# Two filler groups of an attention and soft-MoE kernel divided otherwise: one matmul more, and four of 384 columns for twelve of 128

## The chip, the cores and the metric

The kernel runs on one core of one Trainium2 chip. The metric is the device time of one execution in microseconds (us). Five executions of the kernel before have a median of 302.42 us (302.04 to 304.46). One execution was taken with the hardware profiler as well.

## The reference

What must be computed is an attention over 8 batches of 12 heads (448 tokens, 64 numbers per head) with soft-capped scores, whose output goes into a soft mixture of experts:

```python
scores = cap * np.tanh(scale * np.matmul(q, k.transpose(0, 1, 3, 2)) / cap)      # cap = 30
attn = np.exp(scores - np.max(scores, axis=-1, keepdims=True))
x = np.matmul(attn / np.sum(attn, axis=-1, keepdims=True), v)                    # then tokens x 768
logits = x @ phi                                                                 # 3584 x 32 slots
d = softmax of logits over the tokens;  slot_input = d.T @ x
slot_out[e] = np.maximum(slot_input[e] @ w1[e], 0.0) @ w2[e]                     # 8 experts
c = softmax of logits over the slots;   out = c @ slot_out
```

(The softmaxes are written out in the reference; here they are told in words.) Nothing of the change touches any of these results.

## The kernel before

**Tiles and chunks.** Two heads make a pair, so there are 48 pairs; each pair has 7 key tiles, which makes 336 tiles. The main loop runs over j from 0 to NCH - 1, with NCH = 56, and each j handles a chunk of 6 tiles. For a chunk, TensorE (PE in the profile) makes the scores (`qk_chunk`, L316) into one of two PSUM buffers `sc`; ScalarE (ACT) takes the tanh from there into an SBUF tile `ex` (L325) and later the exponential in place (L329); VectorE (DVE) takes the exponential of one of the six tiles by a polynomial (L362 to L367). Two chunks later TensorE multiplies with the values (`pv_mms`, L385), and VectorE divides by the sums (`norm`, L392 and L395). GpSimd (POOL) casts the values (L286) and issues the loads of weights.

**Who sets the order.** The order on each engine is written out by hand. Every j has slots named by letters: pv_first (the first four key tiles of a pair), slot "a", pv_tail, scores of the next chunk, slot "b", pv_rest with the norm, slot "c", the second half of the next scores, slot "d". A table `aux` holds what is to be called in each slot, and `at(j, slot, f, ...)` (L542) enters a call. TensorE then takes its instructions strictly in that order.

**Fillers.** Some slots hold matmuls whose result nobody reads. `spare(n, parts)` (L547 to L549) takes a tile named `junk` in the PSUM bank that the product with the values uses as well (pool `psV`, one buffer, tag "pv"), and calls `busy` (L625 to L632):

```python
    def spare(n, parts=3):
        busy(n, psV.tile([P, parts * P], F32, name="junk", tag="pv"))
...
        if home.shape[-1] > P:
            for _ in range(n // 3):
                pe.matmul(home, ones, wide, start=True, stop=True)    # L629: 384 columns
            n, home = n % 3, home[:, 0:P]
        for _ in range(n):
            pe.matmul(home, by, by, start=True, stop=True)            # L632: 128 columns
```

So n counts blocks of 128 columns: with parts = 1 each block is a matmul of its own, with parts = 3 three blocks go into one matmul of 384 columns and the remainder into single ones. Each matmul comes with a weight load of its own. Since `junk` and `pv` share one buffer, the fillers must wait until VectorE has read the pair before (`norm`), and the next pair's product must wait until the fillers have left their results.

**Near the end of the loop.** Line 608 enters three such groups: 8 blocks in slot "d" of j = 50, 8 in slot "d" of j = 52, 12 in slot "d" of j = 54, all with parts = 1. In each, pv_first of the next j follows. After j = 54 no scores are left to be made: j = 55 has pv_first, slot "a", pv_tail and pv_rest of pair 45, and then the loop is left. The rest of the attention follows outside the loop: the products of pairs 46 (`pvm`) and 47 (`pvl`), the logits of the last batch (`lpl`), the slot sums (`slpl`). Then come the first expert layer (`hp`, L823), the second (`so_ps`, L856), whose weights are partly read back from DRAM (`w2t`, L802, on the queue of SyncE, SP), and the output (`op`, L892 and L939; stores L872).

Of the kernel before, what the change touches and what calls it, by code (L numbers as in the profile page):

```python
# [36 lines left out]
def kernel(  # L37
# [27 lines left out]
    NCH = NTILE // CH  # L65
# [476 lines left out]
    def at(j, slot, f, *a):  # L542
        if j < 0:
            j, slot = 0, "b"
        aux.setdefault((j, slot), []).append((f, a))
# [21 lines left out]
    for b in range(B):  # L567
        j, p = b * PER, 6 * b
# [36 lines left out]
        at(1 + n * (NCH - 5) // len(wjobs), "b", *job)  # L605
    for j, slot, n in ((0, "a", 10), (0, "c", 10), (1, "b", 10), (1, "c", 8)):
        at(j, slot, spare, n, 1)
    for j, slot, n, parts in ((NCH - 6, "d", 8, 1), (NCH - 4, "d", 8, 1), (NCH - 2, "d", 12, 1)):
        at(j, slot, spare, n, parts)
    at(0, "c", init_vbd, 0)  # L610
    at(1, "c", init_vbd, 1)
# [376 lines left out]
```

## Time and profile before

| what | value |
|---|---|
| median of five executions | 302.42 us (302.04 to 304.46) |
| the profiled execution: its own time | 302.04 us |
| the profiled execution: its span, first to last instruction | 300.1 us |
| mean granted TensorE clock over the span | 0.984 |
| busy: PE / ACT / DVE / POOL | 266.0 / 265.6 / 237.5 / 138.8 us |
| matmuls into `junk` of 128 columns (L632), of 384 columns (L629) | 75 and 63 |
| group of j = 50: first and last start | 227.38 and 227.78 us |
| group of j = 52: first start | 236.45 us |
| group of j = 54: first and last start | 245.49 and 246.11 us |

The profiled execution's own time is 1.94 us more than its span, which is what lies before the first and after the last instruction. A time in us with two decimals in the text below is counted from the start of the span. A busy time is the sum over the span, so it is an average over stages with different limits; which engine sets the time in one stage is read from the chain of waits and from the waits in that stage. In the timelines, a row merges neighbouring instructions of one kind: start, duration of the whole row, engine, line, operation, tiles and the number of instructions; brackets tell how long the engine was idle before and what ended that.

### The profile page before, as it was taken

What the parts mean: (1) busy time and instruction counts of PE and PEld (TensorE: products, weight loads), DVE (VectorE), ACT (ScalarE), POOL (GpSimd) and SP (SyncE); (2) the same over time, 40 slices, a digit from 0 to 9 for tenths busy, and PEclk for the clock granted to TensorE, in tenths of its full rate; (3) what the DMA queues carried; (4) which work ended last, traced back from release to release, by engine and by line L of the source; (5) the groups of instructions that cost most, each with busy time, mean ns of one, the idle gap of its engine ahead of it and who ended that gap; (6) DMA issues with size and microseconds to landing.
All of it is one profiled execution on the core that took longest, in us unless ns stands there. A gap on an engine that the chain in (4) does not pass through costs nothing.

```text
span 300.1 us, 11045 instructions
## 1 busy us (share of the span) xinstructions
PE 266.0 (89%) x4828; PEld 179.3 (60%) x4828; DVE 237.5 (79%) x497; ACT 265.6 (89%) x211; POOL 138.8 (46%) x200
## 2 busy tenths in 40 slices
PE   7898989998999999989999999899999999998710
PEld 5655556755675667566757675667666777542400
DVE  3728989898999999999899999998998864247830
ACT  4999999999999999999999999999999996237720
POOL 4583553764576456645674557465643220300000
PEclk9999999999999999999999999999999999999985
DMA  7999999999999999999999999999999479939995
GB/s 229 254 187 206 208 192 211 178 207 223 226 186 200 201 230 207 192 204 228 168 188 216 229 204 209 214 223 200 197 193 221 122 244 319 404 117 383 411 420 232
DMA packets 58560, 68.14 MB, mean 227 GB/s; under 512 B 4240, under 2 KB 54672, under 8 KB 58512
## 3 DMA queue, kind: packets, MB, share of 16 engines
q0 software_dynamic: 42448, 35.31, 76.5%
q1 hardware_dynamic: 15776, 31.89, 30.5%
q8 instruction: 38, 0.62, 0.8%
q10 hardware_dynamic: 288, 0.23, 0.2%
q14 instruction: 10, 0.08, 0.1%
HBM read 91.72 MB, written 19.27 MB: 370 GB/s over the span
## 4 chain that ended last, share of the span: by engine, by line
ACT 38%; PE 33%; DVE 14%; issue 6%; POOL 2%; DMA 2%; DVEq 0%; SPq 0%; ACTq 0%
ACT ex L325 23%; ACT ex L329 12%; PE pv L385 10%; PE sc L316 5%; DVE xq L395 3%; POOL vbd L286 2%; PE so_ps L856 2%; PE hp L823 2%; PE kps L276 2%; PE qps L276 1%; PE pv L415 1%; DVE work L364 1%; PE xps L433 1%; DVE work L362 1%; DVE work L366 1%
## 5 line engine op out<-in xcount | busy, mean ns | idle before, releaser
L325 ACT ACTIVATE ex<-sc 128x1344 bf16<-128x1344 f32 (+1 forms) x113 | 165.9, 1737 | 1.2 <-PE sc L316 1.2
L329 ACT ACTIVATE ex<-ex 128x2240 bf16<-128x2240 bf16 (+4 forms) x58 | 145.1, 2531 | 0.1
L385 PE MATMUL pv<-vbd,ex 128*128 128x130 bf16 (+1 forms) x1610 | 94.8, 211 | 8.6 <-POOL vbd L286 7.5
L385 PEld LDWEIGHTS <-ex 128*128 128x128 bf16 (+1 forms) x1680 | 76.0, 101 | 31.8 <-issue 9.1
L316 PE MATMUL sc<-qT,kT 64*64 64x448 bf16 x672 | 70.1, 359 | 2.4 <-ACT ex L325 1.8
L286 POOL CAST vbd<-vraw 64x896 bf16<-64x896 f32 x46 | 44.9, 975 | 50.8 <-PE pv L385 36.9
L366 DVE SCALAR_TENSOR_TENSOR work<-work 128x448 f32<-128x448 f32 x51 | 31.8, 623 | 1.2
L367 DVE SCALAR_TENSOR_TENSOR ex<-work 128x448 bf16<-128x448 f32 x51 | 31.9, 625 | 0.6
L365 DVE SCALAR_TENSOR_TENSOR work<-work 128x448 f32<-128x448 uint16 x51 | 31.7, 621 | 0.0
L395 DVE TENSOR_TENSOR xq<-pv,rec 128x448 bf16<-128x448 f32 x46 | 28.7, 625 | 1.6
L316 PEld LDWEIGHTS <-kT 64*64 64x64 bf16 x672 | 24.2, 105 | 7.6 <-issue 5.5
L477 POOL COPY e<-E 128x512 bf16<-128x512 bf16 x9 | 7.0, 778 | 42.9 <-PE eps L496 20.0
L364 DVE TENSOR_SCALAR work<-work 128x448 uint16<-128x448 uint16 x51 | 25.7, 504 | 0.4
L116 POOL DMA_DIRECT2D w1b<-in_moe_w_dram x32 | 24.6, 770 | 0.0
L294 POOL MEMSET vbd<- 64x1 bf16 x22 | 3.3, 149 | 43.1 <-PE pv L385 43.1
L362 DVE TENSOR_SCALAR work<-ex 128x448 int32<-128x448 bf16 x51 | 21.0, 411 | 2.1
L415 PE MATMUL pv<-ones 128*128 128x57 bf16 x502 | 20.8, 188 | 0.0
L278 DVE COPY kT<-kps 128x896 bf16<-128x896 bf16 x23 | 14.2, 618 | 7.4 <-PE kps L276 7.3
L186 POOL DMA_DIRECT2D qb<-in_q_dram x22 | 16.7, 760 | 3.4 <-DVE kT L237 3.4
L415 PEld LDWEIGHTS <-ones 128*128 128x128 bf16 x502 | 17.4, 96 | 0.4
L278 DVE COPY qT<-qps 128x896 bf16<-128x896 bf16 x23 | 14.3, 624 | 3.9 <-PE qps L276 2.9
L446 DVE COPY xT<-xps 128x896 bf16<-128x896 bf16 (+1 forms) x24 | 14.4, 600 | 3.5 <-PE xps L438 3.5
(130 smaller groups left out, 331.5 us busy)
## 6 DMA issues: line engine op xcount, KB each, us to landing
w1b<-in_moe_w_dram POOLq DMA_DIRECT2D x32, 384.0 KB, 8.4
vraw<-in_v_dram SPq DMA_DIRECT2D x44, 224.0 KB, 6.1
w2d<-in_moe_w_dram POOLq DMA_DIRECT2D x21, 384.0 KB, 8.8
w2t<-w2d SPq DMA_DIRECT2D x21, 384.0 KB, 5.6
out_dram<-ob SPq DMA_DIRECT2D x7, 768.0 KB, 8.3
qb<-in_q_dram POOLq DMA_DIRECT2D x22, 224.0 KB, 7.8
kb<-in_k_dram POOLq DMA_DIRECT2D x22, 224.0 KB, 6.4
out_dram<-obh SPq DMA_DIRECT2D x23, 192.0 KB, 2.1
```

Of the source, the lines that this page charges most:

```text
L278: dve.tensor_copy(t, ps)
L286: pool.tensor_copy(vbds[Q % 2][r, :, :, c0:c0 + DH], raw[r])
L316: pe.matmul(sc[cs, u, 0:S], qkT["k", Q][r, c, cs], qkT["q", Q][r, :, cs], start=True, stop=True)
L325: act.activation(exs[j][:, half * CS + u0:half * CS + u1, :], sc[:, u0:u1, 0:S], ACT.Tanh, scale=qk_scale / cap)
L329: act.activation(exs[j][:, u0:u1, :], exs[j][:, u0:u1, :], ACT.Exp, scale=cap)
L364: lambda: dve.tensor_scalar(b.bitcast(U16), w, 7, None, ALU.logical_shift_left),
L365: lambda: dve.scalar_tensor_tensor(p, f, p2, f, ALU.add, ALU.mult),
L366: lambda: dve.scalar_tensor_tensor(p, p, p1, f, ALU.add, ALU.mult),
L367: lambda: dve.scalar_tensor_tensor(t, p, p0, b, ALU.add, ALU.mult))
L385: pe.matmul(out_, exs[j][r, u, q0:q0 + (HP if tail else P)], v_, start=(c == 0 and g == gs[0] < NF), stop=(c == NT - 1), skip_group_check= ...
L395: dve.tensor_tensor(xq[Q][:, h, s0:s1, :], pv[:, 0:s1 - s0, 0:DH], rec.to_broadcast([P, s1 - s0, DH]), op=ALU.mult)
L415: pe.matmul(home, ones, ones[:, 0:512 - NT * W], start=False, stop=True, skip_group_check=True)
```

## The change

One line of the program is altered, in two of its three entries:

```diff
-    for j, slot, n, parts in ((NCH - 6, "d", 8, 1), (NCH - 4, "d", 8, 1), (NCH - 2, "d", 12, 1)):
+    for j, slot, n, parts in ((NCH - 6, "d", 9, 1), (NCH - 4, "d", 8, 1), (NCH - 2, "d", 12, 3)):
         at(j, slot, spare, n, parts)
```

The group of j = 50 gets a ninth matmul of 128 columns: one weight load and one matmul more. The group of j = 54 has 12 blocks as before, but in four matmuls of 384 columns instead of twelve of 128: eight weight loads and eight matmuls fewer. Together that is 14 instructions fewer on TensorE. The tile `junk` of that group is three times as wide, in the same bank. The instructions of VectorE, ScalarE, GpSimd and SyncE, their order and their waits are the same as before; the first filler of the group of j = 54 waits for VectorE, and the first product behind each group waits for TensorE's own results, in both kernels.

## The prediction

> **What bounds the kernel now.** I read the page first, for the shares, then the chain of waits in order of time around the two edited places, then the timelines of ScalarE and of TensorE there, and last the busy times by stretch up to the end.
>
> ```profile
> span 300.1 us, 11045 instructions
> PE 266.0 (89%) x4828; PEld 179.3 (60%) x4828; DVE 237.5 (79%) x497; ACT 265.6 (89%) x211; POOL 138.8 (46%) x200
> ```
>
> TensorE and ScalarE are equally full (266.0 and 265.6 us), so the page alone doesn't say which of them a filler delays. The chain of waits does (columns: start, duration, engine, tile and line):
>
> ```profile
> 227.29 0.15 PE xps L438 x2
> 227.44 0.57 PE junk L632 x8
> 228.01 0.04 issue
> 228.05 0.84 PE pv L385 x12
> ...
> 230.99 0.08 PE pv L385 x3
> 231.07 0.08 issue
> 231.14 0.94 POOL vbd L286
> 232.10 0.85 PE pv L385 x12
> ...
> 244.56 0.22 DVE rec L392
> 244.80 0.64 DVE xq L395
> 245.44 0.05 issue
> 245.49 0.86 PE junk L632 x12
> 246.35 0.04 issue
> 246.39 0.85 PE pv L385 x12
> ```
>
> Both groups are links of the chain that ended last. Between them no link belongs to ScalarE: the chain is TensorE's own sequence, broken by VectorE (244.56 to 245.44) and GpSimd (231.14 to 232.08), both of which start when a TensorE result is there. So whatever moves TensorE at 227.4 moves it at 245.5 as well. After 246.4 it is TensorE again, with one norm at 248.55, up to the first expert layer. ScalarE doesn't idle, but it doesn't hold TensorE either:
>
> ```profile
> 244.22 2.00 ACT L325 ACTIVATE ex<-sc 128x1344 bf16<-128x1344 f32 x1
> 245.39 3.16 ACT L329 ACTIVATE ex<-ex 128x2688 bf16<-128x2688 bf16 x1
> 247.73 2.00 ACT L325 ACTIVATE ex<-sc 128x1344 bf16<-128x1344 f32 x1
> 248.90 3.35 ACT L329 ACTIVATE ex<-ex 128x1344 bf16<-128x1344 bf16 x3
> ```
>
> Its last exponential ends at 252.25. The five products that need it are the last of the 30 `pvl` matmuls that run from 252.19 to 254.15, spaced about 0.06 us, so they are reached some 1.5 us after their data. TensorE has that much room to become earlier before ScalarE is the limit. The other way, a later TensorE would hurt at once, by its own sequence.
>
> **What the Trainium skill says.** Three places bear on this, all of its page "TensorE: Matmul & The Clock Gate". Its section "Back-to-back issue gap" gives a start-to-start distance of N/2.4 + 2.5 ns for N columns at the full clock: 56 ns for 128 and 162.5 ns for 384. The trace agrees: in both old groups the fillers start 55 to 56 ns apart, and 384-column fillers elsewhere (L629 at 216.52) 162 to 163 ns apart; the first step of a group is longer (66 and 174 ns). "Single matmul latency" gives (398 + N)/2.4 ns, 219 and 326 ns; the trace has 219 and 326 as the medians of the two kinds. "Part 1: The HAM clock gate (the "warmup" mystery)" says that the clock is halved after about one window of 3.4 us in which the array is idle. In this trace the granted clock is 1.00 throughout the attention and up to 286.7, and 0.50 only after TensorE has ended.
>
> **The change, part by part.** Fillers stream the same kind of data either way, so I count in columns and in matmuls.
>
> *Ninth filler at j = 50.* One more start at the distance of its neighbours: +0.056 us. Its weight load is pulled beside the filler before (the eight loads of this group lie within 227.37 to 227.82, under the matmuls). What waits behind it is the first product of the next pair, which starts at 228.05 because it needs the last filler's result to have left (275 ns after its start, which is the 219 ns of its duration and some 56 ns of waiting). So it moves by the full 0.056. Behind it the cast at 231.14 waits for TensorE, and TensorE for the cast (0.19 us idle at 232.10); both shift together. Is it hidden anywhere on the way to 245.49? The only idle of TensorE there waits for work that TensorE itself released, so I take +0.056; the ends are 0 (some wait that the profile puts down to the wrong engine covers it) and +0.07 (the first step's distance).
>
> *Four for twelve at j = 54.* Before: first filler at 245.49, first product at 246.39, so 0.900 us, of which 0.624 lie from the first to the last start (66 ns and ten times 56 ns), and 0.276 from the last start to the product. After, with the distances of the group of four at 216.52: 174 + 162 + 163 = 499 ns to the last start, and then 326 ns for the longer matmul plus the same 57 ns of waiting: 0.882 us. That is -0.018 us. The columns are the same 1536, so the array streams as long as before; what is saved is eight times 2.5 ns of distance between matmuls, and the longer last matmul moves the whole of its own extra length into the tail. The eight weight loads that go lie beside matmuls (0.67 us of loads in 245.49 to 246.2) and give nothing more. The ends: +0.02, if the first wide one starts slower, and -0.90, if the group cost nothing at all.
>
> *What doesn't change.* No other engine gets or loses an instruction or a wait, no DMA is moved, and no queue is passed. The wait that sets the group's start (VectorE's norm, 0.40 us of TensorE idle at 245.49) stays. What lies behind the group is pair 45's product, its norm (VectorE at 248.55), and the read-back of `w2t`, which began at 243.20, before the group, and whose data have landed by about 264, while the second layer reads without a wait for them. The output stage is a transfer stage:
>
> ```profile
> 266.00:268.00 2.00, 1.75 (x35) 0.83 (x25) 0.38 (x2) 0.73 (x2) 0.00 (x0) 1.00 0.04 8
> 272.00:274.00 2.00, 1.76 (x21) 0.44 (x13) 1.06 (x3) 1.58 (x3) 0.00 (x0) 1.00 1.05 392
> 282.00:284.00 2.00, 1.19 (x7) 0.58 (x6) 1.57 (x3) 1.38 (x3) 0.00 (x0) 1.00 1.02 422
> 292.00:296.00 4.00, 0.00 (x0) 0.00 (x0) 0.00 (x0) 0.00 (x0) 0.00 (x0) 0.50 1.01 422
> ```
>
> The DMA engines (last two columns: busy share and GB/s) are almost empty before the first store at 268.03 and full from 272 to 296, so the end follows the first stores, and these follow TensorE's chain: a shift at 246 arrives at the end one to one.
>
> *Sum.* +0.056 - 0.018 = +0.04 us. Against the profiled execution's own time: 302.04 + 0.04 = 302.08 us (span 300.1 + 0.04, and the same 1.94 around it). That execution is 0.38 us under the median of the five; put on the median, 302.42 + 0.04 = 302.5 us.
>
> **The rivals.** A measurement of this kernel can tell about 0.5% from no change, 1.51 us: under 300.9 is faster, over 303.9 slower.
>
> *A, the forecast:* 302.5 us. For it speak the distances, which the same trace shows for both widths, and that no wait is added.
>
> *B, slower: the granted clock falls for a window.* The place is the thinnest stretch of the attention, where TensorE is busy 1.60 of 2 us (244 to 246) and 1.66 of 2 (248 to 250), just around the altered group. If dividing the fillers otherwise put one window of 3.4 us under the monitor's bar, a window at half the clock would do 1.7 us less work, on the chain: 302.5 + 1.7 = 304.2 us. It decides from the point at which the monitor counts too little activity; the profile doesn't show that bar, but at 282 to 284 the clock is still granted in full with TensorE busy 1.19 of 2, well under the altered stretch, and the streamed columns don't fall (12 blocks remain 12, and j = 50 gains one). One of the five executions stands at 304.46, so something of that size can happen to this kernel. Little speaks for its happening because of the change.
>
> *C, faster: the group of j = 54 costs far less than its distances say.* If four wide matmuls were free, 0.90 us would go: 302.5 - 0.9 = 301.6, still within 0.5%. To be beyond, the idle of 0.40 us ahead of it and the 0.34 us ahead of `xps` at 249.47 would have to go as well (0.90 + 0.40 + 0.34 = 1.64, 300.8 us), though both wait for VectorE's norm, which nothing shortens. Against it: four such matmuls took 0.82 us at 216.52.
>
> That the change doesn't do what it says is no rival: the 14 instructions fewer are in the built program.
>
> **How the numbers follow.** A 0.77, B 0.14, C 0.09. Of C, where the gain reaches from 0.9 to 1.64 us, I put two thirds beyond 0.5% (0.06) and one third within. B's 304.2 is for a whole window on the chain, and all of it counts as slower. That gives faster 0.06, same 0.80, slower 0.14. The predicted time is A's, 302.5. The range goes down to 301.5, where the free group of C ends (302.42 - 0.90), and up to 303.8, which takes A with the spread of the executions; it leaves out B and the far part of C, 0.20 together. The unknown ends of the two edits (0 to +0.07, and -0.90 to +0.02) lie inside.
>
> **What would show it.** In the profile of the changed kernel: nine fillers of L632 at about 227.4, spaced 56 ns, with the product behind them 0.06 us later; four of L629 at about 245.5, spaced about 163 ns, each 326 ns, and the product 0.88 us after the first; a wait for VectorE ahead of the group as before, about 0.4 us; ScalarE still without idle up to 252.3; the first store at 268.1; granted clock 1.00 up to about 286.7. The prediction is wrong if the clock drops earlier, if TensorE waits in 246 to 258 for something that it didn't wait for before, or if the span differs by more than 1.5 us while these rows agree: then the time is made where I have looked for nothing, in the transfers at the end.

## The result, and the profile after

The changed kernel takes 300.87 us in the median (300.21 to 303.65, 43 runs), the kernel before in the same measurement 302.14 us (80 runs). The ratio is 0.9957, 95% interval 0.9946 to 0.9969: 1.3 us faster, where +0.04 was forecast and 301.5 was the lower end of the range.

The profiled execution took 301.26 us, its span is 299.2. First the two edited places, in the chain of waits of the changed kernel in order of time (start, duration, engine, tile and line):

```profile
227.21 0.62 PE junk L632 x9
227.84 0.04 issue
227.88 0.84 PE pv L385 x12
...
245.26 0.05 issue
245.31 0.84 PE junk L629 x4
246.15 0.04 issue
246.19 0.84 PE pv L385 x12
```

Both are still links of the chain, and both cost what their distances said. The chain's row at j = 50 begins with the second filler; in the timeline the first one starts at 227.15, so from the first filler to the product it is now 0.73 us (before, from 227.38 to 228.05, 0.68: +0.06). At j = 54 it is 0.88 us (before 0.90: -0.02). The wide fillers start 172, 163 and 162 ns apart and last 326 ns. The first store is issued at 267.98, before at 268.03, and the chain's last work on VectorE stands here:

```profile
286.37 0.66 PE op L939 x3
287.03 0.02 issue
287.06 1.02 DVE ob L946
288.07 0.92 DVEq L983
```

Before, that last copy started at 287.11. The two executions differ by up to 0.23 us at places on the way (227.15 against 227.38 already ahead of the first edited group), but from the first store to the last copy they are within 0.06 us of each other. So the span's difference is made after the last copy, while only the stores are still running. The busy times by stretch show it (the last two columns are the busy share of the DMA engines and GB/s). The kernel before:

```profile
295.00:296.00 1.00, 0.00 (x0) 0.00 (x0) 0.00 (x0) 0.00 (x0) 0.00 (x0) 0.50 0.99 409
296.00:297.00 1.00, 0.00 (x0) 0.00 (x0) 0.00 (x0) 0.00 (x0) 0.00 (x0) 0.50 0.66 264
297.00:298.00 1.00, 0.00 (x0) 0.00 (x0) 0.00 (x0) 0.00 (x0) 0.00 (x0) 0.50 0.09 36
298.00:299.00 1.00, 0.00 (x0) 0.00 (x0) 0.00 (x0) 0.00 (x0) 0.00 (x0) 0.50 0.03 12
```

The changed kernel:

```profile
296.00:297.00 1.00, 0.00 (x0) 0.00 (x0) 0.00 (x0) 0.00 (x0) 0.00 (x0) 0.50 0.79 316
297.00:298.00 1.00, 0.00 (x0) 0.00 (x0) 0.00 (x0) 0.00 (x0) 0.00 (x0) 0.50 0.04 14
298.00:299.00 1.00, 0.00 (x0) 0.00 (x0) 0.00 (x0) 0.00 (x0) 0.00 (x0) 0.50 0.00 0
```

In both, nearly all stores have landed by about 297. One engine of sixteen is a share of 0.06, so what is left behind that is the work of one engine or two: before, the packets' own times have the last ones following each other every 0.117 us, as on a single engine, until 298.56; now the last ends at 297.28. The landings of the last store say the same. There are sixteen of them: before, fourteen had come by 297.09, one came at 297.91 and one at 298.89; now fifteen have come by 297.25 and one comes at 298.05. One is late in both, but the last of all comes 0.84 us earlier, which is the difference of the spans (300.05 and 299.21). What the DMA engines carried more before is in the page's list of DMA queues. The kernel before, and then the changed one:

```profile
DMA packets 58560, 68.14 MB, mean 227 GB/s; under 512 B 4240, under 2 KB 54672, under 8 KB 58512
...
q8 instruction: 38, 0.62, 0.8%
```

```profile
DMA packets 58559, 68.12 MB, mean 228 GB/s; under 512 B 4240, under 2 KB 54672, under 8 KB 58512
...
q8 instruction: 37, 0.61, 0.8%
```

One packet less in all, and it is one of queue 8, kind "instruction": 16 KB. The experiments below show that these are TensorE's own instructions: their number and times move with the number of TensorE's instructions alone. In the trace of before the 38th starts at 286.33 and takes 0.93 us, in the midst of the stores; in the trace after, the last one is the 37th, at 267.77, when the engines are almost empty. The Trainium skill has both halves of this: "Runtime: NRT & Kernel Launch", section "Instruction fetch mechanics", says that an engine's instructions are refilled in blocks of 16 KiB, 256 instructions, by a DMA queue of the sequencer's own; "DMA: Bandwidth & Descriptors", section "Queues, rings and completion order", says that each DMA engine takes turns between its queues, packet by packet. The first agrees with the trace (9686 TensorE instructions in the program and 38 fetches, 255 for each). The second can't be read from these traces: their packets don't name their engine, so that the fetch and the late end of the stores are on the same engine is inferred from the times, not shown. The first page adds that the cost of crossing a block's boundary is "mostly hidden"; here the stores beside the fetch pay for it.

### The profile page after: what moved, and what is told of

It reads as the page before. It is cut to its first block, busy times and chain, and to the rows that moved or that the text cites. A ratio compares the mean times of both kernels' runs of the same rounds, so it can differ in the third digit from the quotient of the medians.

```text
span 299.2 us, 11031 instructions
## 1 busy us (share of the span) xinstructions
PE 266.4 (89%) x4821; PEld 179.1 (60%) x4821; DVE 237.4 (79%) x497; ACT 265.6 (89%) x211; POOL 138.8 (46%) x200
## 4 chain that ended last, share of the span: by engine, by line
ACT 39%; PE 34%; DVE 14%; issue 6%; POOL 2%; DMA 1%; DVEq 0%; ACTq 0%
ACT ex L325 23%; ACT ex L329 12%; PE pv L385 10%; PE sc L316 5%; DVE xq L395 3%; POOL vbd L286 2%; PE so_ps L856 2%; PE hp L823 2%; PE kps L276 2%; PE op L939 2%; PE qps L276 2%; PE pv L415 1%; DVE work L364 1%; PE xps L433 1%; DVE work L362 1%
```

## The experiments

Theory 1: the gain is the one fetch that no longer falls among the stores. Theory 2: it is the new shape of the fillers and what follows from their place on the chain. Theory 3: it comes from the ninth filler. The number of TensorE instructions in the program is given for each kernel; before has 9686, the changed one 9672 (each trace has records of two fewer). The filler entries of j = 0 and j = 1 stand at L606 (10, 10, 10 and 8 blocks in single matmuls); moving blocks between single and wide matmuls there changes the number of instructions, far from the end, at nearly the same streaming time.

**e1, the ninth filler alone (9688).**

```diff
-((NCH - 6, "d", 8, 1), (NCH - 4, "d", 8, 1), (NCH - 2, "d", 12, 1))
+((NCH - 6, "d", 9, 1), (NCH - 4, "d", 8, 1), (NCH - 2, "d", 12, 1))
```

> The kernel before with the ninth filler at j = 50 alone: 2 TensorE instructions more than before. Theory 1 (the gain is one 16 KB fetch of TensorE's instructions less, which in the trace of before falls at 286.33 us among the last stores): the fetch is still there, 38 fetches, no gain, +0.06 us of chain, ratio 1.000 to 1.001. Theory 2 (the gain comes from where the fillers stand and how the later transfers fall, a shift of the chain): this part costs +0.06 us, so the same ratio; the run is the control for the others. Theory 3 (the gain is this part's, by a wait that the ninth filler covers): ratio 0.996.

Measured: 302.32 us, ratio 1.0005 (0.9987 to 1.0023), 38 fetches, the last at 284.44. Theory 3 falls.

**e2, the wide group alone (9670).**

```diff
-(NCH - 2, "d", 12, 1)
+(NCH - 2, "d", 12, 3)
```

> The kernel before with the four wide fillers at j = 54 alone: 16 TensorE instructions less than before. Theory 1: 37 fetches, the whole gain, ratio 0.995 to 0.997. Theory 2: the whole gain too, if it is this part that shifts the chain. Theory 3: no gain, 1.000.

Measured: 301.18 us, ratio 0.9964 (0.9942 to 0.9986), 37 fetches. The gain belongs to this part; Theories 1 and 2 both allow that.

**e3, the kernel before with 14 instructions less at the start (9672).**

```diff
-    for j, slot, n in ((0, "a", 10), (0, "c", 10), (1, "b", 10), (1, "c", 8)):
-        at(j, slot, spare, n, 1)
+    for j, slot, n, parts in ((0, "a", 10, 3), (0, "c", 10, 1), (1, "b", 10, 1), (1, "c", 7, 1)):
+        at(j, slot, spare, n, parts)
```

> The kernel before with both groups near the end untouched, and 14 TensorE instructions less in the first 10 us of the loop: ten fillers of 128 columns at j = 0, slot a, put into three wide ones and one, and one filler less at j = 1, slot c. Theory 1: 37 fetches, the whole gain, ratio 0.995 to 0.997, and no last straggling stores after 297.4 us. Theory 2: the groups at the end are as before, so no gain: 0.999 to 1.001.

Measured: 301.01 us, ratio 0.9966 (0.9943 to 0.9989), 37 fetches within the span. The whole gain is there with the two edited groups untouched. Its last stretch is empty from 297 on:

```profile
296.00:297.00 1.00, 0.00 (x0) 0.00 (x0) 0.00 (x0) 0.00 (x0) 0.00 (x0) 0.50 0.32 128
297.00:298.00 1.00, 0.00 (x0) 0.00 (x0) 0.00 (x0) 0.00 (x0) 0.00 (x0) 0.50 0.00 0
```

**e4, the changed kernel with 14 instructions more at the start (9686).** The six fillers ahead of the loop and the four at j = 2 as single matmuls, and one filler more at j = 1.

```diff
-    spare(6)
+    spare(6, 1)
...
-            at(j + 2, "d", spare, 4)
+            at(j + 2, "d", spare, 4, 1)
...
-(1, "c", 8)
+(1, "c", 9)
```

> The changed kernel with 14 TensorE instructions added early: the six fillers ahead of the loop and the four at j = 2 as single ones of 128 columns instead of wide ones, and one filler more at j = 1, slot c. It has as many TensorE instructions as the kernel before, and the change at j = 50 and j = 54 is in it. Theory 1: 38 fetches again, the gain is gone, ratio 0.999 to 1.002. Theory 2: the gain stays, 0.995 to 0.997.

Measured: 302.12 us, ratio 0.9990 (0.9971 to 1.0010), 38 fetches, the last at 286.14. The gain is gone with the change in place. Theory 2 falls.

**e8, the kernel before with 8 instructions less at the start (9678).**

```diff
-    for j, slot, n in ((0, "a", 10), (0, "c", 10), (1, "b", 10), (1, "c", 8)):
-        at(j, slot, spare, n, 1)
+    for j, slot, n, parts in ((0, "a", 10, 1), (0, "c", 10, 1), (1, "b", 10, 1), (1, "c", 8, 3)):
+        at(j, slot, spare, n, parts)
```

> The kernel before with 8 TensorE instructions less, early (the eight fillers of j = 1, slot c, as two wide ones and two single ones). Theory 1: the last fetch is due at a fixed place in the instructions, about 14 before the end of the kernel before, so 8 less don't take it away: 38 fetches, the last of them some 8 instructions nearer to the end, no gain, ratio 0.999 to 1.001. A gain in proportion to the instructions would be 8/14 of the whole, 0.9975.

Measured: 302.10 us, ratio 1.0000 (0.9978 to 1.0021), 38 fetches, the last at 287.99. So the gain is a step, between 9678 and 9672 instructions. The traces show why: the 38th fetch starts when TensorE has begun 9673 of its 9684 recorded instructions in the kernel before, 9673 of 9676 in e8, and all 9670 in e3. There it shows at 299.88, with the closing instructions, when the stores have landed.

At 9672 instructions the fetch is not gone, then, and it isn't always free. In the kernels with that number (changed, e3, e6, e7, e11, e12), 22 of 98 executions have more than 2.2 us outside their span, up to 3.25; in the other kernels no execution has more than 2.03. In the profiles this time grows with how long after the span the 38th fetch starts: 2.01 us at 1.0 us after it (e11), 3.05 at 2.35 (e6). That the fetch is the cause was not tried.

**e5, the changed kernel with 76 instructions less still (9596).** The fillers of L606 as 9, 9, 9 and 6 blocks with parts = 3, and those of j = 50 and j = 52 as 9 blocks with parts = 3.

```diff
-((NCH - 6, "d", 9, 1), (NCH - 4, "d", 8, 1), (NCH - 2, "d", 12, 3))
+((NCH - 6, "d", 9, 3), (NCH - 4, "d", 9, 3), (NCH - 2, "d", 12, 3))
```

> The changed kernel with 76 TensorE instructions less still: the early fillers of j = 0 and 1, and the groups of j = 50 and 52, put into wide matmuls of 384 columns. Theory 1a (a fetch costs when it falls among the stores of the output, and one fetch less is worth nothing by itself): 37 fetches as in the changed kernel, but the last one comes 76 instructions later in the program, at about 270.5 to 271 us, when the transfers are already full; the store that shares its DMA engine ends late, the gain is lost, ratio 0.999 to 1.001. Theory 1b (each fetch less gains, wherever it falls; or fewer instructions are better): ratio 0.996 or lower.

Measured: 301.90 us, ratio 1.0002 (0.9988 to 1.0017), 37 fetches, the last at 271.87, in the stores. So fewer instructions aren't better by themselves: the last fetch is in the full stretch and no longer in the empty one, and the gain is gone. The run isn't clean, though. Its profiled execution (302.80, 0.9 above its median) also has 0.53 us of TensorE idle in the first expert layer, with no releaser in the profile, and its first store only at 268.85. What speaks for the fetch are the late last packets in the table below, and that from the first store on the execution takes as long as those of the other kernels with a fetch in the stores.

**e9, the kernel before with 44 instructions more at the start (9730).**

```diff
-            at(j + 1, "d", spare, 34)
+            at(j + 1, "d", spare, 34, 1)
```

> The kernel before with 44 TensorE instructions more, early (the 34 fillers of j = 1 as single ones instead of eleven wide ones and one). Theory 1a (a fetch costs wherever in the store stage it falls): 38 fetches, the last 44 instructions earlier in the program, at about 280 to 282 us; the store that shares its DMA engine ends late as before: ratio 0.999 to 1.001. Theory 1c (only a fetch near the very end costs, since an earlier one is made up for by the other DMA engines): 0.996. And the last fetch but one moves away from the stores, to about 266 us.

Measured: 301.66 us, ratio 0.9977 (0.9961 to 0.9994), 38 fetches, the last at 279.52, lasting 1.44 us. The median agrees with neither forecast: some 0.7 us were gained, about half of the step (the interval reaches from 0.2 to 1.2 us). The profiled execution, 0.5 above the median, shows none of it: its output stage is as long as before (32.00 us in the table below). It shows no single late engine, but a hole in the stores just behind the fetch:

```profile
278.00:280.00 2.00, 1.96 (x14) 1.11 (x12) 1.30 (x4) 1.95 (x3) 0.57 (x1) 1.00 1.07 392
280.00:282.00 2.00, 1.70 (x19) 0.97 (x18) 2.00 (x4) 1.10 (x3) 0.04 (x1) 1.00 0.31 111
282.00:284.00 2.00, 1.42 (x8) 0.64 (x7) 1.30 (x3) 1.38 (x2) 0.00 (x0) 1.00 1.07 414
```

The kernel before has a share of 1.08 at 280 to 282. ScalarE and VectorE then wait 0.9 and 0.7 us for stores to land before they can write again (before: nothing like it, 0.3 us on an earlier store alone). So a fetch at this place doesn't show as one late engine; whether and how it comes to a smaller cost, one execution doesn't settle.

**e7, the changed kernel without the groups of j = 50, 52 and 54 (9672).** The line of the change is removed; the 34 fillers of j = 1 are single ones and j = 1, slot "c" has 7, so that the number of instructions stays.

> The changed kernel without the three groups of j = 50, 52 and 54, with as many TensorE instructions as the changed kernel (the 34 fillers of j = 1 as single ones, and one filler less at j = 1, slot c). If all three lie on the chain: 0.66 + 0.61 + 0.88 = 2.15 us earlier at most, and ScalarE, whose last exponential has some 1.5 us of room, cuts that to about 1.5 us: ratio against before 0.990 to 0.991. If only the last lies on the chain: 0.993. If the clock falls: over 1.000.

Measured: 299.60 us, ratio 0.9922 (0.9903 to 0.9942), 37 fetches: faster than both kernels. TensorE's clock didn't fall: it is granted in full up to the output. The chain of waits now comes over ScalarE up to the end of its exponentials:

```profile
243.16 1.96 ACT ex L329
245.12 1.18 ACT ex L325
246.30 2.34 ACT ex L329
248.64 0.05 issue
248.69 1.30 PE pvm L385 x25
```

**e10, e7 with 14 instructions more at the start (9686).** `spare(6, 1)`, `spare, 4, 1` and 8 in place of 7 blocks, as in e4.

> The kernel without the three groups, with 14 TensorE instructions more than in that run, early: as many as the kernel before. Theory 1: the 38th fetch comes back among the stores, and with it 1.3 us: about 300.9 us, ratio 0.996 to 0.997, against 0.992 without it. If the fetch only cost because the chain stood as in the kernel before: 0.992.

Measured: 301.13 us, ratio 0.9961 (0.9942 to 0.9979), 38 fetches. The fetch costs its step here too, 0.0039 of the ratio or 1.2 us, with another chain ahead of it.

**e6 and e12, the changed kernel without the group of j = 54, and e11, the changed kernel once more (9672 each).**

```diff
-(NCH - 4, "d", 8, 1), (NCH - 2, "d", 12, 3))
+(NCH - 4, "d", 8, 1))
...
-            at(j + 2, "d", spare, 4)
+            at(j + 2, "d", spare, 4, 1)
...
-(1, "c", 8)
+(1, "c", 10)
```

> The changed kernel without the group of j = 54 (no filler there), with 8 TensorE instructions put in early so that it has as many as the changed kernel. If the group lies on the chain to the end, as the prediction has it: first product of pair 45 0.88 us earlier, the first store 0.9 us earlier, 37 fetches, ratio against before 0.9957 - 0.0029 = 0.993. If the chain's shifts don't arrive at the end: 0.996. If TensorE's clock falls: over 1.000.

> The changed kernel once more, as the measure for the next run on the same chip: ratio 0.9957, 37 fetches.

> The changed kernel without the group of j = 54, with as many TensorE instructions, once more beside the changed kernel. If the 0.88 us of the group arrive at the end one to one: 0.9 us under the changed kernel, ratio against before 0.993. If part of it is lost behind the attention: between 0.993 and 0.9957, as in the first run of it (0.995).

Measured: e6 300.67 us, ratio 0.9950 (0.9935 to 0.9964); the second time, as e12, 300.51 us, 0.9933 (0.9907 to 0.9959), beside e11 on the same chip with 301.22 us, 0.9956 (0.9937 to 0.9976). Side by side the group is worth 0.7 us of the 0.88 that the chain shows at 246; the first run gave less, 0.2 against the changed kernel's own measurement. The first store comes earlier without the group (267.24 in e6 and 266.86 in e12, against 267.98), so it lies on the path to the output. How much of its length arrives at the end is not shown: the intervals of e11 and e12 overlap.

**The late engine, over the runs.** From the packets' own times in the traces (us; one profiled execution each): the start of the last instruction fetch, the end of the twentieth-last data packet of the stores, the end of the last one, and the difference of these two. The last column is the time from the issue of the first store to the end of the span, which leaves out whatever came before the output.

| kernel | last fetch | twentieth-last | last | difference | first store to end of span |
|---|---|---|---|---|---|
| before | 286.33 | 296.70 | 298.56 | 1.86 | 32.02 |
| e1 | 284.44 | 297.09 | 298.98 | 1.89 | 31.96 |
| e4 | 286.14 | 296.45 | 298.36 | 1.91 | 32.05 |
| e8 | 287.99 | 296.68 | 298.60 | 1.92 | 32.01 |
| e10 | 289.05 | 298.20 | 300.13 | 1.93 | 32.04 |
| e5 | 271.87 | 297.60 | 299.36 | 1.76 | 32.03 |
| e9 | 279.52 | 298.21 | 298.66 | 0.45 | 32.00 |
| changed | 267.77 | 296.75 | 297.28 | 0.53 | 31.23 |
| e11 | 266.93, then after the stores | 296.49 | 296.81 | 0.32 | 30.74 |
| e2 | 267.23 | 297.12 | 297.45 | 0.33 | 30.75 |
| e3 | 267.45, then after the stores | 296.27 | 296.75 | 0.48 | 30.94 |
| e6 | 267.50, then after the stores | 296.24 | 296.73 | 0.49 | 31.43 |
| e12 | 266.38, then after the stores | 295.53 | 296.10 | 0.57 | 31.15 |
| e7 | 266.21, then after the stores | 295.24 | 295.64 | 0.40 | 30.86 |

With a fetch among the stores the last packet ends 1.8 to 1.9 us behind the rest (e9 apart), without one 0.3 to 0.6, some 1.4 us less. Not all of that arrives at the end, since without a fetch another landing is the last one. What arrives is in the last column: about 32.0 us in every execution with a fetch among the stores, and 30.7 to 31.4 us, 31.0 in the mean, in every one without. So the stage of the stores alone is about 1.0 us shorter without the fetch; the medians of whole executions gained 1.0 (e2) to 1.3 us (the change), and the intervals don't tell these apart.

## Why the prediction was wrong

- **What bounds the kernel** was right. Both groups lie on TensorE's chain and stayed on it; e7 shows that ScalarE is the limit right behind, after about 1.1 us (0.9957 - 0.9922 of 302); the prediction had read some 1.5 us of room.
- **The ninth filler**, forecast +0.056: measured +0.06 in the profile; e1's 1.0005 (0.9987 to 1.0023) is too coarse to tell it from nothing.
- **Four for twelve**, forecast -0.018: measured -0.02.
- **"What doesn't change"** is the step that failed. It says that no DMA is moved and no queue is passed, because it counted the DMAs that the program issues, and so it put the transfers at the end at nothing; what the runs showed is that the end of these transfers gave the gain (1.3 us in the medians, about 1.0 us in the stage of the stores). The instructions themselves are transfers. Fourteen of them less take TensorE's program under the point at which its 38th block is fetched during the stores. The page of before had the row (38 packets on queue 8) and the trace had the time, 286.33; the prediction reads neither.
- **"The end follows the first stores"** holds for the stores' bulk (twentieth-last packet 296.70 before, 296.75 after, first stores 268.03 and 267.98), not for the last packet, which is what ends the execution. A share of 0.09 at 297 to 298 and 0.03 at 298 to 299 was there to be read in the kernel before: an engine or two of sixteen, alone. The prediction's last sentence did name the transfers at the end as the place where it had looked for nothing, but none of its chances and no part of its range stood for them.
- **The clock** stayed in full, as forecast, but the prediction's 286.7 for its end is misread: in the kernel before it is granted in full until 290.3, in the changed one until 290.7.
- **The rivals.** B didn't happen, and e7 argues against it in this stretch: with 29 blocks of fillers less the clock stayed up. C had the right side but the wrong cause, since the four wide matmuls cost just what was forecast. Its bound, that a gain can't exceed what stands around the group, was one on TensorE's time only.

## What to carry to other kernels

These are lessons from one kernel. Where a kernel ends in a stretch with all DMA engines full, count everything that uses them there, the engines' own instructions included, and look at which engine's last packet ends the run. An edit that adds or takes instructions can move a fetch of the whole engine's stream into or out of that stretch, wherever in the program it is made; here the effect was a step and not a slope, and in e5 it came back when the fetch before reached the stretch. To see what an edit itself is worth, hold the number of instructions and measure again: here the edit was worth nothing that could be measured (e4: 0.9990, 0.9971 to 1.0010), and its count 1.0 to 1.3 us, while removing the fillers at an equal count was worth 1.1 us more.

## What the runs showed of the hardware that was not expected

- A 16 KB fetch of instructions took about 0.95 us in the median of every trace (0.88 to 1.53) and no longer than that at most places among the stores (0.93 before), but among the stores it made the output stage about 1.0 us longer (32.0 us against 31.0).
- In the first expert layer TensorE is idle once, for 0 to 0.7 us from execution to execution (0.18 before, 0.13 after, none in e3's and e7's; 0.53 in e5's and 0.72 in e2's, there with no releaser in the profile). Its cause wasn't tried.
- In e10's profiled execution (303.56 us, against a median of 301.13) TensorE ran slower up to about 13 us: score matmuls of 448 columns lasted 577 ns where e7's lasted 349, and the chain was 2.4 us late by then and stayed so. The trace's record of the clock granted in full begins at 13.43 us there, against 3.6 to 6.3 us in all other traces. Some executions of the kernel before are 2.2 us and more above its median too (304.3 to 305.1); whether from the same cause, no trace shows.
